# Second expert stream started at the middle expert, and the gates' power issued early in its step

## The chip, the cores and the metric

The kernel runs on one core of one Trainium2 chip. The metric is device time in microseconds of that core, the median of several executions. For the kernel before, three executions took 743.41, 747.35 and 751.59 us; the median is 747.35 us.

## The reference, cut to what matters

Chunked attention makes x, and a router with one expert for each token (top 1) is applied to it.

```python
# attention: q, k, v are (8, 8, 576, 64); chunks of 64 keys, softmax inside a chunk
x = attn_out.transpose(0, 2, 1, 3).reshape(4608, 512)
# router and experts: w1 is (8, 512, 1024), w2 is (8, 1024, 512)
logits = norm(x) @ norm(expert_emb).T / tau
expert_idx = argmax(logits, axis=1)
gate_w = softmax(logits)[row, expert_idx]
for e in range(8):
    mask = expert_idx == e
    out[mask] = gate_w[mask, None] * (relu(x[mask] @ w1[e]) @ w2[e])
```

With the inputs that are used, the experts 0 to 7 get 832, 359, 183, 448, 512, 1023, 576 and 675 tokens. In groups of G = 64 tokens, the last of an expert filled up, that is 13, 6, 3, 7, 8, 16, 9 and 11 groups, 73 in all. These counts were worked out from the reference, not read from a trace.

## The kernel before, in words

**First phase.** Attention, logits and the choice of the expert run tile by tile (128 tokens). Every token's row, with its logits, its squared norm and its number, is scattered to a table `spots` in DRAM, in which each expert has a stretch of its own.

**Second phase, in steps.** A step j takes two groups of 64 tokens, one of each of two streams: stream 0 in partitions 0 to 63, stream 1 in 64 to 127. In the first NE = 4 steps both streams take groups at the start of one expert's stretch, fixed in the program: expert 0 for stream 0 and expert E-1 = 7 for stream 1 (`load_first`, `first_rows`, and `ends_e`, which marks the two experts whose first four groups are done). All groups left over, in the order of their experts, are then walked from both ends: stream 0 from the first upwards, stream 1 from the last downwards (`groups`, `places`). For stream 1, `e_0` is the expert of the first four steps, and `swap` at step 4 is set where the expert of step 4 is another. With the counts above stream 0 walks its experts 0, 1, 2, 3, 4 and changes at steps 13, 19, 22 and 29; stream 1 walks 7, 6, 5 and changes at steps 11 and 20. There are 36 steps of two groups and one of a single group (`step_alone`).

**One step.** The two matrix products of a step are done with seven block products in place of eight. `hidden_fast(j)` (L394) makes the first (L408, products p1 to p7, in six PSUM banks that are reused in turn), with the sums of results on VectorE (`add`, L438), the ReLUs on ScalarE (L425) and the 32x32 transposes on VectorE (`turn`, L432). `result_fast(j)` (L466) makes the second (L485), adds on VectorE (L499), scales by the gate on ScalarE (L511) and scatters the rows to the output from GpSimd (`put_rows`, L543). The sums of x and of h that the seven products need are made by GpSimd (`add_x`, `add_h`, L377).

**The loop (L1267).** The loop's turn j, called turn j below, issues `hidden_fast(j + 1)` and inside it, through `middle()`, `result_fast(j)`. The callbacks fix the order on every engine: `first()` after p1, then a copy of p1 on ScalarE (L442, once a turn, a good clock of the turns), `then()`, p2, `turn_next()` (transposes x of step j+2, issues the loads of step j+4), the other products, and `middle()` after the last of them.

**Changing the expert.** The products use `w1_sb`, `w2_sb` and three sums of weight blocks for each stream (`sums_sb`, `sums2_sb`). The next expert's weights wait in `next_w1` and `next_w2`. For a change at step J, `take_next(J)` in turn J-2 (inside `change`, which `middle` calls last) and `take_next2(J, s)` bring the new weights into use: each has copies on ScalarE (L341, L350), three subtractions of 128x1024 on VectorE and one on GpSimd (L333); `take_next2` has one GpSimd copy more (L353). `take_next2` runs in turn J-1 for stream 0 (inside `change`), and in turn J for stream 1 (inside `then`). All of it stands under run-time conditions (`tc.If`, L339, L348, L359), whose flags each engine loads and tests. After the loop's turn in which `next_w1` was taken, `load_behind(n, next_w1, ...)` (L192, L1323) fetches the weights that come after; `then` does so for `next_w2`. These are loads of 2 MB with a run-time condition, in SyncE's queue, in which the loads of x and of `spot2` stand too.

**Gates.** For every four steps j, j+1, j+2, j+3 with j a multiple of 4, `gates_of_four(j)` (L242) makes the gates in four parts: a power on GpSimd (L254, 128x8) that reads the `spot2` slots of the four steps, five VectorE instructions (L256 to L262), an exponential on ScalarE (L264), and four VectorE instructions (L266 to L269). `middle()` issues the first two parts, before `change(j)`; the rest comes after `hidden_fast`.

Of the kernel before, what the change touches and what calls it, by code (L numbers as in the profile page):

```python
# [13 lines left out]
ALU = mybir.AluOpType  # L14
# [11 lines left out]
def kernel(  # L26
# [11 lines left out]
    nc = tc.nc  # L38
    B, H, S, Dh = q.shape
    E, D = moe_expert_emb.shape  # L40
# [7 lines left out]
    G = P // 2  # L48
# [5 lines left out]
    NE = 4  # L54
# [7 lines left out]
    GB = 4  # L62
# [64 lines left out]
    def load_first(buf, rows):  # L127

        for s in range(2):
            e = (0, E - 1)[s]  # L130
            nc.sync.dma_start(out=whole(buf[s]), in_=rows[:, e : e + 1, :], max_dma_last_dim=4096)

    xin, mo = {}, {}

    def number(ap, top, *engines):
# [34 lines left out]
    def load_x(j):  # L174
        rows = []
        for s in range(2 if j != LEAST else 1):
            row = number(src_row[of_step(s, j)], SPARE, ENG.SP)
            rows.append(spots[ds(row, G), :])
        load_rows(j, rows)

    def first_rows(s, j, n):
        r0 = (0, E - 1)[s] * R + G * j
        return spots[r0 : r0 + G * n, :]

    def load_when(w, rows, e, f):
# [6 lines left out]
    def load_behind(j, place, rows):  # L192

        c = LEAST - 2 - j
        for s in range(2):
            at = (slice(G * s, G * s + 1), slice(c, c + 1))
            load_when(place[s], rows, after[at], more_e[at])
# [44 lines left out]
    def gates_of_four(j):  # L242

        i0 = j % SPOTS2
        sp = spot2[:, i0 : i0 + GB].rearrange("p j b e -> p (j b) e")
        n = 2 * GB
        wide = [P, n, E]
        rn, lmax, sh = g_rn, g_max, g_sh
        place = (j // GB) % 2
        gate, at2 = gates2[:, place], at2s[:, place]  # L250
        for i in range(GB):
            at = slice(2 * i, 2 * i + 2)
            gate_of[j + i] = gate[:, at], at2[:, at]
        nc.gpsimd.tensor_tensor(rn, sp[:, :, SQ], half, ALU.pow)  # L254
        yield
        nc.vector.tensor_reduce(lmax, sp[:, :, 0:E], axis=AX.X, op=ALU.max)  # L256
        nc.vector.tensor_scalar(rn, rn, 1e-6, None, ALU.add)
        nc.vector.reciprocal(rn, rn)
        nc.vector.tensor_tensor(
            sh, sp[:, :, 0:E], lmax.unsqueeze(2).to_broadcast(wide), ALU.subtract  # L260
        )
        nc.vector.tensor_tensor(sh, sh, rn.unsqueeze(2).to_broadcast(wide), ALU.mult)  # L262
        yield
        nc.scalar.activation(sh, sh, AF.Exp)  # L264
        yield
        nc.vector.tensor_reduce(gate, sh, axis=AX.X, op=ALU.add)  # L266
        nc.vector.tensor_scalar(gate, gate, 1e-9, None, ALU.add)
        nc.vector.reciprocal(gate, gate)
        nc.vector.tensor_scalar(at2, sp[:, :, TOK].bitcast(I32), 2.0, odd_q, ALU.mult, ALU.add)  # L269
# [291 lines left out]
    with (  # L561
# [63 lines left out]
        def constant_parts():  # L625
            nc.gpsimd.iota(io_i, pattern=[[1, NST]], base=0, channel_multiplier=0)
            nc.gpsimd.iota(part_i, pattern=[[0, 1]], base=0, channel_multiplier=1)
            nc.gpsimd.memset(blank, 0.0)
            nc.gpsimd.memset(blank[:, D + TOK : D + TOK + 1].bitcast(I32), NO_ROW)
            yield  # L630
            make_upper_triangular(nc, sltb, val=1.0, diag=False)
            nc.gpsimd.memset(onesb, 1.0)
            nc.gpsimd.tensor_copy(io, io_i)
            nc.gpsimd.tensor_copy(at, part_i)
            yield
            nc.gpsimd.tensor_scalar(pref, io[:, 0:E], -1.0, float(E), ALU.mult, ALU.add)
            nc.gpsimd.tensor_scalar(e_base, io[:, 0:E], float(R), None, ALU.mult)
            nc.gpsimd.memset(before, 0.0)
            nc.gpsimd.memset(eqb_all[:, 0], 0.0)
            nc.gpsimd.memset(ones, 1.0)  # L640
            yield
            nc.gpsimd.memset(jump[:, 1], 1.0)
            nc.gpsimd.memset(nb[:, 0:1], float((SPARE + R) // G))
            yield
            nc.gpsimd.tensor_scalar(second, at, float(G), None, ALU.is_ge)
            nc.gpsimd.tensor_scalar(is_0, at, 2.0, None, ALU.is_lt)
            yield
            nc.gpsimd.tensor_scalar(lim, at, -float(P), float(G * NE), ALU.mult, ALU.add)
            nc.gpsimd.tensor_scalar(step, second, -2.0, 1.0, ALU.mult, ALU.add)
            yield  # L650
            nc.gpsimd.tensor_scalar(first_s, second, -1.0, 1.0, ALU.mult, ALU.add)
            nc.gpsimd.tensor_scalar(back, io, -1.0, float(NST - 1), ALU.mult, ALU.add)
            yield
            nc.gpsimd.tensor_scalar(more_g, back, float(LEAST - NE), None, ALU.is_ge)
            nc.gpsimd.tensor_scalar(pair_g, back, float(LEAST - NE), None, ALU.is_equal)
            yield
            nc.gpsimd.tensor_tensor(more_g, more_g, pair_g, ALU.add)
            nc.gpsimd.tensor_tensor(pair_g, back, more_g, ALU.subtract)
            yield
            nc.gpsimd.memset(more_e[:, NSW - 1 : NSW], 1)  # L660
            nc.gpsimd.tensor_scalar(e_0, second, float(E - 1), None, ALU.mult)
            yield
            nc.gpsimd.tensor_scalar(e_1, e_0, 1.0, None, ALU.add)
            nc.gpsimd.tensor_scalar(ends_e, io[:, 0:E], 0.0, None, ALU.is_equal)
            yield
            nc.gpsimd.tensor_scalar(full, io[:, 0:E], float(E - 1), None, ALU.is_equal)
            nc.gpsimd.tensor_tensor(ends_e, ends_e, full, ALU.add)
            yield
            nc.gpsimd.tensor_scalar(done, ends_e, float(NE), None, ALU.mult)
            nc.gpsimd.tensor_scalar(ends_e, ends_e, is_0, None, ALU.mult)  # L670
            yield
            nc.gpsimd.tensor_scalar(in_g, second, -float(G), at, ALU.mult, ALU.add)
            nc.gpsimd.tensor_scalar(odd_q, in_g, float(Q), None, ALU.is_ge)
            nc.gpsimd.tensor_scalar(e_p, second, float(R), None, ALU.mult)
            yield
            nc.gpsimd.tensor_scalar(
                base_h, io[:, 0 : E // 2], 2.0 * R, e_p, ALU.mult, ALU.add
            )
# [564 lines left out]
    spot2 = late_p.tile([P, SPOTS2, 2, E + 2], FP32, name="spot2")  # L1243

    load_x(NE)

    with (
        tc.tile_pool(name="ps_h", bufs=1, space=PSUM, reuse_waits="tile") as ps_h,
# [18 lines left out]
        for j in range(LEAST - 1):  # L1267
            n = j + 2

            def first():  # L1270
                next(ended, None)

            def then():
                if NE <= j:
                    take_next2(j, 1)
                    load_behind(j, next_w2, w2_rows)

            def turn_next():
                next(ended, None)
                if n <= LEAST:  # L1280
                    turn_xb(n)
                if n < LEAST and n + XBUF < NJ:
                    load_x(n + XBUF)

            def middle():
                nonlocal ended, four
                if n < LEAST:
                    add_x(n)
                if NE <= j:
                    if j % GB == 0:  # L1290
                        four = gates_of_four(j)
                        next(four)
                        next(four)
                    ended = result_fast(j, ps_y)
                    next(ended)
                change(j)

            if j == 0:
                first_parts()
                add_up(0, None, TS)  # L1300
                first_parts()
            elif j == 1:
                turn_next()
                add_x(n)
                add_up(1, None, TS)
                hidden_plain(2, w1_sb, lambda s: add_up(s, None, ("T3",)))
            else:
                hidden_fast(j + 1, ps_h, first, then, turn_next, middle)
                for _ in four:
                    pass  # L1310

            if j < NE:
                result(j, ps_y)
                if j >= 2:
                    add_up(j - 2, None, TS, block2)
                if j == NE - 1:
                    for s in range(2):
                        add_up(s, None, ("T3",), block2, nc.gpsimd)
                    take_next2(NE, 0)
            if by_sevens(j + 1):  # L1320
                add_h(j + 1)
            if NE - 1 <= n < LEAST - 1:
                load_behind(n, next_w1, w1_rows)  # L1323
            elif n == LEAST - 1:
                load_late(LEAST, next_w1, w1_rows)
            if j == 1:
                load_behind(NE - 1, next_w2, w2_rows)
# [78 lines left out]
```

## Time and profile before

| what | value |
|---|---|
| median of three executions | 747.35 us |
| the profiled execution | 704.9 us |
| its span, first to last instruction | 703.0 us |
| mean granted TensorE clock in it | 0.965 |
| busy: TensorE matmul / VectorE / ScalarE / GpSimd | 88% / 67% / 53% / 60% |
| start of L442 in turn 2 / in turn 34 | 203.1 / 661.7 us |
| weight loads issued by SyncE (L188), with a condition each | 134 |

A line of a view names start, duration, engine, source line, operation, output and inputs; in brackets stands how long the engine was idle before it and what ended that. In the view of waits, each line names who waited for whom, then the total in us, the number of times and the longest. The sequencer of an engine is written with a q (DVEq): waiting, branching and issuing are its work. DVE is VectorE, ACT ScalarE, PE TensorE, POOL GpSimd, SP SyncE.

### The profile page before, as it was taken

The numbers are of one execution on the slowest core, as the hardware profiler recorded it, in microseconds if no ns is written. First come the engines' busy times: TensorE is split into PE (matmuls) and PEld (weight loads), VectorE is DVE, ScalarE is ACT, GpSimd is POOL, SyncE is SP. The second block draws the span as 40 slices with busy tenths as digits, with TensorE's granted clock in tenths as the row PEclk, the third lists the DMA queues.
The fourth block names the chain that finished last, engine by engine and source line by source line (L and its number), as shares of the span: only waits on it lengthen the run. The fifth ranks groups of instructions, "written<-read, shape, count | busy, mean of one in ns | idle before, by whom it ended". The sixth has DMA issues, their size and how long they took to land. (4 is left out here: it accounts for less than half of the span.)

```text
span 703.0 us, 36397 instructions
## 1 busy us (share of the span) xinstructions
PE 619.4 (88%) x14864; PEld 502.1 (71%) x14864; DVE 469.4 (67%) x1097; ACT 374.9 (53%) x691; POOL 422.8 (60%) x563
## 2 busy tenths in 40 slices
PE   4989899988999899988869999587899998899981
PEld 3878787875445688766649997463699996689971
DVE  2868788884987465576765667886756675765640
ACT  4657676762135365464636566453564755465630
POOL 5749888723442766456766567774666667555631
PEclk9999999999999999999999999897999999799997
DMA  9989999989349121114732114313331111111111
GB/s 227 231 245 272 263 280 277 299 302 389 102 160 390 41 58 40 40 44 156 276 111 95 41 55 160 133 39 131 106 115 38 55 46 34 34 55 38 35 49 31
DMA packets 95468, 96.52 MB, mean 137 GB/s; under 512 B 57788, under 2 KB 77500, under 8 KB 95272
## 3 DMA queue, kind: packets, MB, share of 16 engines
q1 hardware_dynamic: 83032, 55.86, 26.0%
q0 software_dynamic: 12208, 38.04, 16.5%
q8 instruction: 121, 1.98, 1.2%
q14 instruction: 75, 0.61, 0.3%
q10 hardware_dynamic: 32, 0.02, 0.0%
HBM read 328.21 MB, written 22.69 MB: 499 GB/s over the span
## 5 line engine op out<-in xcount | busy, mean ns | idle before, releaser
L425 ACT ACTIVATE h<-C 64x256 f32<-64x256 f32 x264 | 180.7, 684 | 150.6 <-DVE C L438 142.7
L438 DVE TENSOR_TENSOR C<-C,h 128x256 f32<-128x256 f32 x231 | 93.4, 416 | 58.5 <-ACTq L359 22.2
L543 POOL DMA_INDIRECT out_dram<-y,at2s x64 | 63.5, 992 | 83.4 <-ACT y L511 43.4
L408 PE MATMUL h<-sums,xbT 128*32 128x256 f32 x1056 | 81.7, 385 | 8.8 <-DVEq L339 5.5
L485 PE MATMUL y_ps<-w,hT 128*32 128x128 f32 x2048 | 71.3, 291 | 20.4 <-DVE y L499 20.4
L377 POOL TENSOR_TENSOR S<-hT 128x256 f32<-128x256 f32 x64 | 47.0, 735 | 67.3 <-DVE gates L266 20.4
L485 PEld LDWEIGHTS y_ps<-w,hT 128*32 128x32 f32 x2048 | 65.2, 118 | 26.3 <-DVE y L499 23.8
L408 PE MATMUL h<-w,S 128*32 128x256 f32 x1056 | 80.8, 385 | 2.1 <-POOL S L377 1.6
L485 PE MATMUL y_ps<-w,S 128*32 128x128 f32 x2048 | 76.2, 275 | 4.3 <-POOLq L348 3.1
L432 DVE STREAM_TRANSPOSE hT<-h 128x512 f32<-128x512 f32 x66 | 46.7, 707 | 42.9 <-ACT h L425 34.3
L408 PE MATMUL h<-w,xbT 128*32 128x256 f32 x1056 | 69.6, 385 | 5.5 <-ACT w L341 2.9
L485 PE MATMUL y_ps<-sums,hT 128*32 128x128 f32 x2048 | 67.4, 277 | 2.6 <-DVE sums L333 2.4
L485 PEld LDWEIGHTS y_ps<-w,S 128*32 128x32 f32 x2048 | 64.3, 111 | 6.1 <-POOLq L348 3.9
L499 DVE TENSOR_TENSOR y<-y,y_ps 128x128 f32<-128x128 f32 (+1 forms) x192 | 56.1, 306 | 18.7 <-PE y_ps L485 11.1
L408 PEld LDWEIGHTS h<-sums,xbT 128*32 128x32 f32 x1056 | 45.8, 111 | 28.6 <-issue 8.2
L485 PEld LDWEIGHTS y_ps<-sums,hT 128*32 128x32 f32 x2048 | 61.1, 112 | 3.5 <-DVE sums L333 2.9
L408 PEld LDWEIGHTS h<-w,S 128*32 128x32 f32 x1056 | 47.0, 112 | 19.1 <-POOL S L377 2.6
L408 PEld LDWEIGHTS h<-w,xbT 128*32 128x32 f32 x1056 | 43.6, 111 | 20.3 <-ACT w L341 4.0
L930 POOL DMA_INDIRECT spots<-xr,dest x36 | 37.5, 1041 | 25.7 <-DVE dest L895 8.5
L209 DVE STREAM_TRANSPOSE xbT<-xin 128x256 f32<-128x256 f32 x73 | 45.5, 658 | 0.1
L702 POOL DMA_DIRECT2D kx<-in_k_dram x36 | 32.0, 891 | 19.7 <-PE tr L725 19.1
L408 PE MATMUL h<-sums,S 128*32 128x256 f32 x528 | 42.2, 393 | 0.0
(231 smaller groups left out, 1185.0 us busy)
## 6 DMA issues: line engine op xcount, KB each, us to landing
next_w<-in_moe_w_dram SPq DMA_DIRECT2D x134, 2048.0 KB
xin<-spots SPq DMA_DIRECT2D x154, 64.0 KB
qx<-in_q_dram POOLq DMA_DIRECT2D x32, 256.0 KB
w<-in_moe_w_dram SPq DMA_DIRECT2D x4, 2048.0 KB
v<-in_v_dram SPq DMA_DIRECT2D x56, 144.0 KB
kx<-in_k_dram POOLq DMA_DIRECT2D x28, 256.0 KB
spot<-spots SPq DMA_DIRECT2D x128, 2.5 KB
spots<-blank SPq DMA_DIRECT2D x9, 144.0 KB
```

The source lines that it names most:

```text
L209: nc.vector.transpose(xT[:, :, cols].rearrange("p c (b i) -> p b c i", i=Q), t[:, s * (D // 2) : (s + 1) * (D // 2)].rearrange("p (b i c) ...
L377: nc.gpsimd.tensor_tensor(o, a, b, op)
L408: nc.tensor.matmul(ps[t0 : t0 + Q], lhsT=a[:, c, s], rhs=w[:, r], start=c == 0, stop=c == KD // 2 - 1,)
L425: nc.scalar.activation(h[b][G * v : G * v + G, s].rearrange("p (k i) -> p k i", i=Q), x[G * s : G * s + G].rearrange("p (i k) -> p k i", i=Q),
L432: nc.vector.transpose(hT.rearrange("p k (s b i) -> p b s k i", b=2, i=Q)[:, b], h[b].rearrange("p s (k i) -> p s k i", i=Q),)
L438: nc.vector.tensor_tensor(out, a, b, op)
L485: nc.tensor.matmul(o[t0 : t0 + Q], lhsT=a[:, c, s], rhs=block2(s, m)[:, c, r], start=c == 0, stop=c == KF // 2 - 1,)
L499: nc.vector.tensor_tensor(out, a, b, ALU.add)
L543: ins = nc.gpsimd.indirect_dma_start(out=to, out_offset=bass.IndirectOffsetOnAxis(ap=at, axis=0), in_=y, in_offset=None, bounds_check=boun ...
L702: eng.dma_start(out=x[done : done + n], in_=src[b, :, s : s + n, :].rearrange("h p d -> p h d"),)
L930: ins = nc.gpsimd.indirect_dma_start(out=spots, out_offset=bass.IndirectOffsetOnAxis(ap=at, axis=0), in_=m, in_offset=None, bounds_check=S ...
```

## The change

Three edits, made together. First, the fixed expert of stream 1 becomes E // 2 = 4 wherever E - 1 stood for it. Second, `load_behind(NE - 1, next_w1, ...)` moves from the end of turn 1 to a place ahead of the loop. Third, the generator of the gates is made in `first()`, which issues its GpSimd power there; `middle()` goes on with its VectorE part.

The walk over the left-over groups from both ends stays as it is. Stream 1 now takes four groups of expert 4 and then begins at the last expert, so that with the counts above it walks 4, 7, 6, 5 and changes at steps 4, 15 and 24. Stream 0 walks 0, 1, 2, 3, 4, 5 and changes at steps 13, 19, 22, 29 and 33.

```diff
     def load_first(buf, rows):
         for s in range(2):
-            e = (0, E - 1)[s]
+            e = START[s]
...
+    START = 0, E // 2
...
     def first_rows(s, j, n):
-        r0 = (0, E - 1)[s] * R + G * j
+        r0 = START[s] * R + G * j
...
-            nc.gpsimd.tensor_scalar(e_0, second, float(E - 1), None, ALU.mult)
+            nc.gpsimd.tensor_scalar(e_0, second, float(START[1]), None, ALU.mult)
...
-            nc.gpsimd.tensor_scalar(full, io[:, 0:E], float(E - 1), None, ALU.is_equal)
+            nc.gpsimd.tensor_scalar(full, io[:, 0:E], float(START[1]), None, ALU.is_equal)
...
     load_x(NE)
+    load_behind(NE - 1, next_w1, w1_rows)
...
             def first():
+                nonlocal four
+                if NE <= j and j % GB == 0:
+                    four = gates_of_four(j)
+                    next(four)
                 next(ended, None)
...
             def middle():
-                nonlocal ended, four
+                nonlocal ended
                 if n < LEAST:
                     add_x(n)
                 if NE <= j:
-                    if j % GB == 0:
-                        four = gates_of_four(j)
-                        next(four)
-                        next(four)
+                    next(four, None)
                     ended = result_fast(j, ps_y)
                     next(ended)
                 change(j)
...
-            if NE - 1 <= n < LEAST - 1:
+            if NE <= n < LEAST - 1:
                 load_behind(n, next_w1, w1_rows)
```

## Prediction

> **What bounds the kernel now.** I read the busy shares first: TensorE 88%, VectorE 67%. The loop of turns was therefore to be measured turn by turn, and the copy L442 on ScalarE, one in each turn, gives the clock. Lines of ScalarE's timeline, turns 24, 25, then 28 to 31:
>
> ```profile
> 528.12 0.37 ACT L442 COPY C<-h 128x256 f32<-128x256 f32 x1 [2.29 <-PE h L408]
> 540.28 0.37 ACT L442 COPY C<-h 128x256 f32<-128x256 f32 x1 [0.79 <-PE h L408]
> ...
> 577.86 0.38 ACT L442 COPY C<-h 128x256 f32<-128x256 f32 x1
> 593.47 0.38 ACT L442 COPY C<-h 128x256 f32<-128x256 f32 x1
> 613.08 0.37 ACT L442 COPY C<-h 128x256 f32<-128x256 f32 x1 [1.83 <-PE h L408]
> 625.26 0.37 ACT L442 COPY C<-h 128x256 f32<-128x256 f32 x1 [2.03 <-PE h L408]
> ```
>
> A quiet turn takes 540.28 - 528.12 = 12.16 us, and there TensorE is busy throughout (12.20 of 12.20 us from 528.5 to 540.7). Turns 28 and 29, about the change of stream 0 at step 29, take 15.61 and 19.61. Over all turns from 4 to 33 the excess over 12.16 us is: turn 4, 3.3; turn 8, 1.3; turns 9 and 10, 7.0 (stream 1 changes at 11); turns 11 to 13, 14.5 (the rest of that, and stream 0 at 13); turns 17 to 22, 31.1 (changes at 19, 20, 22); turns 27 to 29, 11.9 (change at 29). That is 69.1 us; the rest of the loop is bound by TensorE. The turns 16, 24 and 32 make gates too and have no excess.
>
> Next, who waits. From the view of waits:
>
> ```profile
> PE y_ps L485 <- DVE y L499: 20.4, 6, 7.2
> DVE g_rn L257 <- POOL g_rn L254: 19.3, 8, 3.3
> ```
>
> TensorE stands still because VectorE is late with y, and VectorE waits 2.4 us for the gates' power, eight times. The timeline about the change at 29 joins the two:
>
> ```profile
> 588.47 0.18 DVE L256 TENSOR_REDUCE g_max<-spot 128x8 f32<-128x64 f32 x1
> ...
> 589.77 1.67 POOL L254 TENSOR_TENSOR g_rn<-spot,halves 128x8 f32<-128x8 f32 x1
> ...
> 591.47 0.17 DVE L257 TENSOR_SCALAR g_rn<-g_rn 128x8 f32<-128x8 f32 x1 [2.82 <-POOL g_rn L254]
> ...
> 595.06 1.49 DVE L333 TENSOR_TENSOR sums<-next_w 128x1024 f32<-128x1024 f32 x1 [2.84 <-DVEq L339]
> ...
> 602.98 3.64 PE L485 MATMUL y_ps<-w,hT 128*32 128x128 f32 x64 [3.37 <-DVE y L499]
> ```
>
> VectorE loses 2.82 us to the power, 2.84 to its conditions, some 4.6 to the three subtractions, and only then makes hT and y. TensorE then waits 3.37 us and runs its next 64 matmuls in 3.64 us, against 1.92 in a quiet turn. Turn 4 is another case, GpSimd late with two first subtractions:
>
> ```profile
> 229.43 4.74 POOL L333 TENSOR_TENSOR w<-w 128x1024 f32<-128x1024 f32 x2
> 234.35 0.72 POOL L377 TENSOR_TENSOR S<-hT 128x256 f32<-128x256 f32 x1 [0.18 <-POOLq L348]
> ```
>
> **What the Trainium skill says.** "TensorE: Matmul & The Clock Gate", section "Part 1: The HAM clock gate", says that the array drops to half clock after an idle window of about 3.4 us; the trace agrees (mean granted clock 0.74 from 593.5 to 613.1, the 64 matmuls above), so a stall costs more than its length. "SBUF — State Buffer", section "SBUF: two separate sides", says that a VectorE instruction with two SBUF inputs and a GpSimd one exclude each other; the trace agrees (L333 takes 1.22 to 3.37 us on VectorE and 2.36 to 3.38 on GpSimd). "Runtime: NRT & Kernel Launch", section "Instruction fetch mechanics", says that a taken branch can force a fetch; the 2.84 us at L339 fit, but no row here shows the cause.
>
> **The change, part by part.** I price it by changes of an expert, and the prices come from the table above.
>
> *Stream 0, with the power early.* The change at 29 cost 11.9. With the power issued in `first`, GpSimd makes it after `add_h`, some 3.4 us into the turn, while it has 5 us free (6.78 of 12.20 busy). VectorE then goes through L257 at once, and its chain to y is 2.8 earlier; TensorE is bound by that chain, so 2.8 is gained whole: 9.1. It can be worked out the other way: y would end at 600.2, where TensorE without the stall at 593.5 would want it at about 595; 5.2 of stall, 2.9 of half clock until 608.7, and 1.0 in turn 27 make 9.1. Where no gates are made in the turn, about 1.9 us less VectorE work (nine small instructions) stands in the way: 7.2. The changes 13, 29 and 33 end in turns 12, 28 and 32 with gates; 19 and 22 do not.
>
> *Stream 1.* `take_next` delays TensorE by 1.35 (copies of w, at 305.0) and then 1.27 (y, at 312.9); with the half of 7.0 that the gates of turn 8 already cost VectorE, I take 4. `take_next2` in `then` made TensorE wait 2.38 at 331.7 for the subtractions, with some half clock: 3.5. Together 7.5. Bounds: 4, if VectorE's spare 5.3 us of a turn (6.87 of 12.20 busy) take most of it, and 10.
>
> *Step 4, new.* The subtractions of expert 4's w2 in turns 3 and 4 are still made, and thrown away. In turn 4 GpSimd has the two first subtractions until 234.2, `add_h` until 237.5, now the power (1.7), the condition (1.1), then `take_next2`'s subtraction (2.4 to 3.3): done at 242.7 to 243.6. TensorE wants it as third product of `result_fast(4)` at about 234.6. The stall is 8 to 9 us against 2.7 before; with 1.7 to 3.4 of half clock behind it, and about 1 from `take_next(4)` in turn 2, where three subtractions delay VectorE by some 5 us, mostly behind the 7.0 us of plain products (L525), turn 4 loses 9.5 more than before. Bounds 5 and 14. The copy of 2.0 us after it hides behind three products of 0.87.
>
> *The load moved ahead.* Two issues of about 1.6 us and 2 x 2 MB at the 415 GB/s seen from 205 to 228 us: landed near 201 us, if the buffers are free at 191. SyncE's queue is passed by nothing but the loads of step 5, whose transposes come at 216.9, and `take_next(4)` reads at about 212: hidden. Without it the weights of step 4 would land at 214 or later. As the weights no longer come as 8 MB in one stretch, x of steps 6 and 7 comes some 10 us earlier, and VectorE's wait of 4.66 at 240.3 for `spot2` goes; it was hidden by GpSimd's lateness in part. Two more changes mean 4 x 2 MB more, at 5 us each beside quiet turns: nothing.
>
> *Waits added.* The power in `first` now waits for `spot2` of step j+3, loaded in turn j-1, and behind it on GpSimd stand `put_rows`, `add_x` and so L408's third product. SyncE is busy for about 11.9 of 12.16 us in a turn, and in turn 8 it was a turn late: `spot2` landed at 290.2, 10.6 into the turn. There GpSimd stands about 6 us and its rows and `add_x` come 0 to 2 us late; against that goes the excess of 1.3. I take 0 left in turn 8; bounds 0 and 3.
>
> Sum of the excess after: turn 4, 3.3 + 9.5 = 12.8; stream 0, 3 x 9.1 + 2 x 7.2 = 41.7, and 1 for the gates in turn 20; stream 1, 2 x 7.5 = 15; 2 more where a change of one stream follows on the tail of the other's (13 to 15, 21 to 24). In all 72.5, against 69.1: 3.4 us more, on the execution of 704.9. The median of the runs is 42 us above that execution, and nothing in the trace tells me where; I add the same 3 us to it: 750 us.
>
> So the split of the streams is worth little by these prices: three changes in turns 17 to 22 cost 31.1, and the prices of single ones would give 11.9 + 7.5 + 9.1 = 28.5. What is gained by the power (8.4 at three changes and 1.3 at turn 8) pays for less than two new changes.
>
> **Rivals.** *The overlap was dear.* If changes that stand alone fall into the spare 5 us of VectorE and 5 of ScalarE, those without gates cost perhaps 4 rather than 7, and the half clock seldom comes. Then 3 x 6 + 2 x 4 + 2 x 4 + 12 = 46, 23 less than before: 725 us. For it: three subtractions at 1.23 are under the spare time. Against it: the change at 29 stood alone. Halfway, 736.
>
> *Step 4 is dear (the other side).* One mechanism: GpSimd in turn 4. If its subtraction meets VectorE's (3.3 rather than 2.4, for all three), it ends at 246, and VectorE's own chain, 5 us late from turn 2, ends after that; stall 11.5, and half clock for 6.8 us. Turn 4 then loses 14 rather than 9.5, and the result is 755; from 13.5 on the kernel is over 1% slower if the other changes stay at their prices of 9.1 throughout (stream 0 at 45.5), which gives 760.
>
> *The change does not do what it says.* If `spot2` is late in turns 8, 16 and 20, the early power holds GpSimd and VectorE waits as before: 8 us worse than my sum, 758. Against it: at 16 and 24 the loads had landed when VectorE asked (it waited for the power alone).
>
> **How the numbers follow.** Little net change (743 to 754): 0.42, with its own range 742 to 755. Dear overlap, whole or half: 0.25, 725 to 740. Dear step 4: 0.20; late loads: 0.13; both reach 755 to 765. About 1%, 7.5 us, is what a measurement tells from no change. Faster by more than that: 0.26; within: 0.38, as part of the first case spills on both sides; slower: 0.36. The range for 8 in 10 is 733 to 765.
>
> **What would show it.** Right: VectorE's wait for L254 falls from 19.3 to near 0; `take_next` at L333 on GpSimd counts 16 rather than 12; turn 4 takes 22 to 28 us with TensorE waiting for POOL at L485; turns 9 and 10 take 12.2; turns 31 to 33 have an excess of 9. Wrong: turn 4 under 19 us, or lone changes at 15, 24 and 33 with an excess under 4 each, or GpSimd waiting over 3 us at L254.

## The result, and the profile after

| what | before | after |
|---|---|---|
| median of 20 runs each | 747.29 us | 751.46 us |
| lowest and highest run | 742.68, 752.26 | 748.39, 755.35 |
| profiled execution, its span | 704.9, 703.0 us | 748.75, 746.8 us |
| mean granted TensorE clock | 0.965 | 0.967 |

The ratio is 1.0056 [1.0031, 1.0081]: within 1%, 4.2 us more, and inside the range. All ratios here are worked out from the fast executions alone, as a few are slow at a lower clock, and so differ by up to about half a point (0.01 of a ratio is a point) from the quotients of the medians. The two profiles, though, are not of one kind, and this has to be read first. ScalarE's timeline of the kernel after, the clock copy (now L445; lines after the first edit moved by three), turns 25 to 27 and then 29 to 31:

```profile
564.92 0.37 ACT L445 COPY C<-h 128x256 f32<-128x256 f32 x1 [1.71 <-PE h L411]
578.33 0.37 ACT L445 COPY C<-h 128x256 f32<-128x256 f32 x1 [2.88 <-PE h L411]
591.71 0.37 ACT L445 COPY C<-h 128x256 f32<-128x256 f32 x1 [2.93 <-PE h L411]
...
621.53 0.38 ACT L445 COPY C<-h 128x256 f32<-128x256 f32 x1
640.85 0.37 ACT L445 COPY C<-h 128x256 f32<-128x256 f32 x1 [2.42 <-PE h L411]
654.32 0.37 ACT L445 COPY C<-h 128x256 f32<-128x256 f32 x1 [2.98 <-PE h L411]
```

A quiet turn takes 13.41 us here (564.92 to 578.33), where the profile of before had 12.16. The view of waits of the same kernel shows in which product the 1.25 us lie (who waited for what, total us, times, longest):

```profile
PE y_ps L488 <- issue: 29.2, 67, 1.2
...
PE y_ps L488 <- DVE y L502: 18.2, 8, 4.3
...
PE y_ps L488 <- POOL w L336: 10.4, 2, 7.7
```

"Issue" means that TensorE waited for nothing that the profile shows. The 29.2 us are less than 33 turns x 1.25 us = 41, but the place is right: in the quiet turn from 578.33 the first 64 matmuls of L488 last from 583.19 to 586.16, 2.97 us, where they take 1.75 in a quiet turn of after_again (551.41 to 553.16), the same kernel on another chip (below). That run has quiet turns of 12.16 us, and in its view of waits stands:

```profile
PE y_ps L488 <- issue: 1.7, 2, 1.0
```

There the kernel before has a median of 708.35 us, 39 less than in the table, against those 41 us. That is the likely answer to what the prediction left open, why the runs took 42 us more than the profiled execution: it was made on another chip than they. This is inferred. The record gives no chip number for the runs of the table, and no profile of the kernel before has turns of 13.4 us; why such turns wait is not known. Turns are compared below between profiles with quiet turns of 12.16 us, unless the text says otherwise.

The lines about the change at step 29, kernel after, its timeline:

```profile
616.34 0.29 DVE L260 TENSOR_SCALAR g_rn<-g_rn 128x8 f32<-128x8 f32 x1
...
620.34 1.23 DVE L336 TENSOR_TENSOR sums<-next_w 128x1024 f32<-128x1024 f32 x1 [2.59 <-PE y_ps L488]
621.04 2.76 POOL L336 TENSOR_TENSOR w<-next_w 128x1024 f32<-128x1024 f32 x1 [2.29 <-DMA spot<-spots]
621.67 5.18 DVE L336 TENSOR_TENSOR sums<-next_w,sums 128x1024 f32<-128x1024 f32 x2
...
630.05 3.64 PE L488 MATMUL y_ps<-w,hT 128*32 128x128 f32 x64 [4.18 <-DVE y L502]
```

VectorE's wait of 2.82 us for the power is gone, but the two later subtractions take 5.18 us, with GpSimd's subtraction (2.76 us) beside them. TensorE still waits 4.18 us for y. Turn 4 of the kernel after, on GpSimd and TensorE:

```profile
241.80 5.89 POOL L336 TENSOR_TENSOR w<-w 128x1024 f32<-128x1024 f32 x2
...
247.88 1.47 POOL L380 TENSOR_TENSOR S<-hT 128x256 f32<-128x256 f32 x1 [0.18 <-POOLq L351]
...
253.43 1.68 POOL L257 TENSOR_TENSOR g_rn<-spot,halves 128x8 f32<-128x8 f32 x1
255.10 2.35 POOL L336 TENSOR_TENSOR w<-next_w 128x1024 f32<-128x1024 f32 x1
...
257.50 1.71 PE L488 MATMUL y_ps<-w,S 128*32 128x128 f32 x26 [7.69 <-POOL w L336]
```

This is the order that was foreseen: first sums, sums of h, power, subtraction, and TensorE standing still for 7.69 us until the last. Turn 4 takes 24.3 us.

### The profile page after: what moved, and what is told of

Read it like the earlier page. It is cut to its first block, busy times and chain, and to the rows that moved or that the text cites. A ratio compares the mean times of both kernels' runs of the same rounds, so it can differ in the third digit from the quotient of the medians.

```text
span 746.8 us, 36513 instructions
## 1 busy us (share of the span) xinstructions
PE 636.8 (85%) x14864; PEld 535.5 (72%) x14864; DVE 504.8 (68%) x1109; ACT 384.7 (52%) x701; POOL 439.7 (59%) x569
## 3 DMA queue, kind: packets, MB, share of 16 engines
q1 hardware_dynamic: 85144, 64.25, 27.7%
## 5 line engine op out<-in xcount | busy, mean ns | idle before, releaser
L441 DVE TENSOR_TENSOR C<-C,h 128x256 f32<-128x256 f32 x231 | 93.4, 416 | 66.7 <-ACTq L362 15.3
L488 PE MATMUL y_ps<-w,hT 128*32 128x128 f32 x2048 | 79.1, 284 | 31.8 <-DVE y L502 18.2
L488 PEld LDWEIGHTS y_ps<-w,hT 128*32 128x32 f32 x2048 | 65.9, 114 | 45.2 <-DVE y L502 22.5
L488 PE MATMUL y_ps<-w,S 128*32 128x128 f32 x2048 | 82.5, 283 | 18.1 <-POOL w L336 10.4
L488 PE MATMUL y_ps<-sums,hT 128*32 128x128 f32 x2048 | 77.2, 277 | 14.3 <-issue 14.2
L488 PEld LDWEIGHTS y_ps<-w,S 128*32 128x32 f32 x2048 | 68.5, 114 | 21.6 <-POOL w L336 10.9
L488 PEld LDWEIGHTS y_ps<-sums,hT 128*32 128x32 f32 x2048 | 64.6, 112 | 22.0 <-issue 21.1
L411 PEld LDWEIGHTS h<-sums,xbT 128*32 128x32 f32 x1056 | 55.1, 110 | 6.5
L336 POOL TENSOR_TENSOR w<-next_w 128x1024 f32<-128x1024 f32 x16 | 48.9, 3054 | 18.2 <-PE h L411 6.9
L411 PEld LDWEIGHTS h<-w,S 128*32 128x32 f32 x1056 | 55.1, 110 | 6.3
L411 PEld LDWEIGHTS h<-w,xbT 128*32 128x32 f32 x1056 | 50.7, 110 | 6.6 <-issue 1.2
L336 DVE TENSOR_TENSOR sums<-next_w,sums 128x1024 f32<-128x1024 f32 x24 | 54.1, 2255 | 1.2
```

The costliest lines, as they stand in the source:

```text
L336: eng.tensor_tensor(of(s, o), of(s, a, w), of(s, b, w), ALU.subtract)
L411: nc.tensor.matmul(ps[t0 : t0 + Q], lhsT=a[:, c, s], rhs=w[:, r], start=c == 0, stop=c == KD // 2 - 1,)
L441: nc.vector.tensor_tensor(out, a, b, op)
L488: nc.tensor.matmul(o[t0 : t0 + Q], lhsT=a[:, c, s], rhs=block2(s, m)[:, c, r], start=c == 0, stop=c == KF // 2 - 1,)
```

## The experiments

The theory going in: each change of an expert has its price, separating the streams saves little, and the two added changes (steps 4 and 33) are paid by the early power. The rival: that the overlap of changes was dear, and the change gained there what it lost elsewhere. Several chips were used, each run beside the kernel before on its own chip (medians 707.8 to 708.4 us, quiet turns of 12.16 us in every profile). The excess is what turns take over 12.16 us each, in one profiled execution.

**before_again**: no edit.

> The kernel before, unchanged, for a second profile of it. In the profile of after a quiet turn takes 13.4 us and TensorE waits some 1.2 us in each for 'issue' at L488; in the profile of before it took 12.16. Theory: that wait belongs to the execution and not to the change, so this profile shows quiet turns of about 13.4 us and a span near 745 us. Rival: the change itself slowed the quiet turns, so this profile shows 12.16 us again and a span near 703 us. The time is about 747 us by either.

716.58 us in one run, beside a median of 707.79, and quiet turns of 12.16 us. The time of 747 us was expected by both theories and did not come. That it is not the change that makes quiet turns long is shown by after_again, below. The excess over turns 4 to 33 is 73.0 us, where the first profile had 69.3; most of the longer time was lost before the loop (turn 2 starts at 210.56 us, not 203.1). A single profile of one kernel thus varies by some 4 us in this sum, and differences below that in one profile prove nothing.

**power_only, split_only, no_idle_sums**, together. The first is the third edit alone on the kernel before:

```diff
             def first():
+                nonlocal four
+                if NE <= j and j % GB == 0:
+                    four = gates_of_four(j)
+                    next(four)
...
             def middle():
...
-                    if j % GB == 0:
-                        four = gates_of_four(j)
-                        next(four)
-                        next(four)
+                    next(four, None)
```

> Only the third edit: the gates' power in first(), with stream 1 still starting at expert 7 and the load where it was. Theory (the sum of the prediction): 2.8 us gained at each of the three changes whose turn makes gates (turns 12, 20, 28) and 1.3 at turn 8, so about 738 us, ratio 0.987. Rival 1 (the power only moves the wait to GpSimd's other work): 747 us. Rival 2 (the gain of the whole change comes from the split, and the power does harm in turns with late loads): over 747 us.

704.38 us, ratio 0.995 [0.9926, 0.9973], where the theory had 0.987. The power early is a gain by itself, but less than half of that expected, as turn 4 takes 22.37 us (16.55 in before_again). Its timeline there:

```profile
243.83 1.68 POOL L254 TENSOR_TENSOR g_rn<-spot,halves 128x8 f32<-128x8 f32 x1 [3.39 <-DMA next_w<-in_moe_w_dram]
245.61 1.71 PE L485 MATMUL y_ps<-w,S 128*32 128x128 f32 x26 [7.12 <-POOLq L348]
```

GpSimd stands 3.39 us; the profile names the load of weights, behind which the rows for the power stand in SyncE's queue. TensorE stands 7.12 us for GpSimd to pass a condition (L348) whose block it does not even enter. The rival of the late loads is real, where the weight load is not moved ahead.

split_only is the first two edits, with the power left in `middle()` (here against the kernel after):

```diff
...
             def middle():
...
                 if NE <= j:
-                    next(four, None)
+                    if j % GB == 0:
+                        four = gates_of_four(j)
+                        next(four)
+                        next(four)
```

> The first two edits without the third: stream 1 starts at expert 4, the load stands ahead of the loop, the power stays in middle(). Theory: two more changes of an expert, less what the overlap had cost, 747 + 13 = 760 us, ratio 1.017; of that about 9 in turn 4. Rival (overlap was dear): the split alone is not slower than before, 740 to 749 us.

724.57 us, ratio 1.0186 [1.0122, 1.025], as expected. no_idle_sums is the kernel after without the first sums of stream 1's second weights, which nothing reads:

```diff
-                if j >= 2:
-                    add_up(j - 2, None, TS, block2)
+                if j == 2:
+                    add_up(0, None, TS, block2)
                 if j == NE - 1:
-                    for s in range(2):
-                        add_up(s, None, ("T3",), block2, nc.gpsimd)
+                    add_up(0, None, ("T3",), block2, nc.gpsimd)
```

> The changed kernel without the first sums of stream 1's second weights (three subtractions on VectorE in turn 3, one on GpSimd), which are overwritten before use as stream 1 changes at step 4 with these inputs. Theory: in turn 4 GpSimd is what TensorE waits for (7.69 us at L488), so the stall shrinks by the 2.4 to 2.9 us of the subtraction and by VectorE's 3.7 us that block it: turn 4 takes about 18 us and not 24, and the time is about 746 us. Rival: VectorE's lateness from turn 2 sets the stall, and turn 4 keeps 22 us or more: 750 us.

718.12 us, ratio 1.0157 [1.0108, 1.0206]; turn 4 takes 21.2 us, between the two that were expected, where the kernel after takes 24.5 (after_again). But the long stall did not shrink, as the theory had it:

```profile
246.18 1.71 PE L488 MATMUL y_ps<-w,S 128*32 128x128 f32 x26 [8.08 <-POOL w L336]
```

It is 7.68 us in after_again. What went are two shorter waits ahead of it, 1.89 and 1.73 us there and 0.35 here. The first sums are part of turn 4's price, not all of it.

**after_again, load_only, power_and_load, start_at_5**, together on a third chip. after_again has no edit.

> The changed kernel, unchanged, so that it can be compared on the chip of these runs. Where quiet turns take 12.16 us, theory: the first prices hold in full, sum of the excess about 72 us against 69 for before, ratio 1.005. But the split alone measured 1.0186 and the power alone 0.995; if these add, 1.0186 - 0.005 = 1.0136. Rival (the early power is worth its full 8 to 10 us only beside the moved load): 1.005.

722.57 us, ratio 1.0217 [1.0176, 1.0259]: 14.2 us more than before, where the table above has 4.2, and more than either expectation (1.0136 and 1.005). The size of the effect differs between the two chips.

load_only is the second edit alone on the kernel before, shown here; power_and_load is the kernel after with `START = 0, E - 1`, that is, the second and third edits:

```diff
     load_x(NE)
+    load_behind(NE - 1, next_w1, w1_rows)
...
-            if NE - 1 <= n < LEAST - 1:
+            if NE <= n < LEAST - 1:
```

> Only the second edit: the load of the next first weights ahead of the loop, power in middle(), stream 1 from expert 7. Theory: VectorE's wait for spot2 in turn 4 goes, but GpSimd is late there all the same, so 0 to 2 us: ratio 0.997 to 1.000. Rival: the late loads are what makes turn 4 long, 4 us and more: 0.994.

705.96 us, ratio 0.9974 [0.995, 0.9998], as expected.

> The second and third edit without the split: stream 1 from expert 7, six changes. With the power alone turn 4 took 22.4 us against 16.6, as GpSimd waited 3.4 us at L254 for spot2 and TensorE 7.1 us for GpSimd. Theory: with the load moved that wait goes and the power gains its whole 8 to 10 us: ratio 0.986 to 0.989, turn 4 about 16 us or less. Rival (the power is worth 0.5% with or without the load): 0.995.

699.82 us, ratio 0.9903 [0.9876, 0.993], though turn 4 takes 18.73 us and not the 16 of the theory. Without the split the change is a gain of about 1%. The split is what costs: 3.1 points beside the other two edits, 2.1 between load_only and split_only, which ran on different chips.

start_at_5 is the kernel after with `START = 0, E // 2 + 1`, so that stream 0 has no change at step 33, while the others stand at 13, 19, 22, 29 and 4, 15, 24 as before:

> The changed kernel with stream 1 started at expert 5 rather than 4. With these inputs stream 0 then walks 0 to 4 and changes at 13, 19, 22, 29, and stream 1 walks 5, 7, 6, 5 and changes at 4, 15, 24: the same schedule as the changed kernel without stream 0's change at 33, and still no two changes in the same turns. Theory (each change has its price): 9 us faster than the changed kernel, ratio 1.2 points under that of after_again; turns 31 to 33 take 12.16 us each. Rival (what counts is that streams change apart; the number of changes is cheap): within 2 us of after_again.

712.1 us, ratio 1.0052 [1.0028, 1.0076]. One change less is 10.5 us less than after_again; the excess of turns 31 to 33 in after_again was 10.4. Now the groups of turns:

| excess, us | turn 4 | 5 to 16 | 17 to 24 | 27 to 29 | 31 to 33 | sum |
|---|---|---|---|---|---|---|
| before_again | 4.4 | 24.5 | 33.3 | 10.8 | 0 | 73.0 |
| load_only | 2.7 | 22.8 | 33.1 | 10.8 | 0 | 69.5 |
| power_and_load | 6.6 | 15.9 | 26.6 | 10.6 | 0 | 59.7 |
| predicted for after | 12.8 | 17.6 | 23.9 | 9.1 | 9.1 | 72.5 |
| split_only | 12.1 | 21.3 | 31.1 | 11.9 | 10.6 | 86.0 |
| after_again | 12.4 | 19.1 | 27.7 | 11.4 | 10.4 | 80.9 |

Three changes stand close in power_and_load (19, 20, 22: 26.6 us) and apart in after_again (19, 22, 24: 27.7); with the power late they cost 33.1 close (load_only) and 31.1 apart (split_only). The rival of the dear overlap, which was to save 23 us, falls.

The early power takes 7 us each from turns 5 to 16 and 17 to 24 where stream 1 starts from expert 7 (load_only against power_and_load). Where it starts from expert 4 (split_only against after_again) it takes 2.1 and 3.5, 5.1 us over all turns, and the two ratios, 1.0186 and 1.0217, show no gain at all. And in neither does it take anything clear of the variation from a change that stands alone, in turns 27 to 29 or 31 to 33. Why not is read in two timelines of one chip, which differ by the third edit. First load_only:

```profile
590.92 0.18 DVE L256 TENSOR_REDUCE g_max<-spot 128x8 f32<-128x64 f32 x1
...
593.92 0.17 DVE L257 TENSOR_SCALAR g_rn<-g_rn 128x8 f32<-128x8 f32 x1 [2.82 <-POOL g_rn L254]
...
595.54 2.35 POOL L333 TENSOR_TENSOR w<-next_w 128x1024 f32<-128x1024 f32 x1 [1.66 <-DMA spot<-spots]
...
597.51 1.46 DVE L333 TENSOR_TENSOR sums<-next_w 128x1024 f32<-128x1024 f32 x1 [2.84 <-DVEq L339]
...
599.08 3.13 DVE L333 TENSOR_TENSOR sums<-next_w,sums 128x1024 f32<-128x1024 f32 x2
602.13 0.70 DVE L432 STREAM_TRANSPOSE hT<-h 128x512 f32<-128x512 f32 x1
```

Then power_and_load:

```profile
585.11 0.18 DVE L259 TENSOR_REDUCE g_max<-spot 128x8 f32<-128x64 f32 x1
585.21 0.28 DVE L260 TENSOR_SCALAR g_rn<-g_rn 128x8 f32<-128x8 f32 x1
...
589.30 1.23 DVE L336 TENSOR_TENSOR sums<-next_w 128x1024 f32<-128x1024 f32 x1 [2.69 <-PE h L411]
...
589.90 2.87 POOL L336 TENSOR_TENSOR w<-next_w 128x1024 f32<-128x1024 f32 x1 [2.30 <-DMA spot<-spots]
...
590.64 5.20 DVE L336 TENSOR_TENSOR sums<-next_w,sums 128x1024 f32<-128x1024 f32 x2
...
595.75 0.70 DVE L435 STREAM_TRANSPOSE hT<-h 128x512 f32<-128x512 f32 x1
...
599.03 3.22 PE L488 MATMUL y_ps<-w,hT 128*32 128x128 f32 x56 [6.14 <-DVE y L502]
```

From the reduction of the gates to the first subtraction VectorE takes 6.59 us with the power late (597.51 - 590.92) and 4.19 with the power early (589.30 - 585.11): 2.4 of the 2.8 us arrive. But with the power late, GpSimd's subtraction began 2 us ahead of VectorE's first, while VectorE waited, and it was done when VectorE's second began. Now it begins inside the first, and VectorE's second and third take 5.20 us rather than 3.13. Of 2.4 us, 2.1 are gone again, and hT, which the next product needs, is made only 0.6 us earlier (10.64 after the reduction, not 11.21).

The kernel after has the same. At the change of step 33, split_only, then after_again:

```profile
664.60 2.36 POOL L336 TENSOR_TENSOR w<-next_w 128x1024 f32<-128x1024 f32 x1 [1.67 <-POOLq L342]
...
668.15 3.12 DVE L336 TENSOR_TENSOR sums<-next_w,sums 128x1024 f32<-128x1024 f32 x2
```

```profile
659.53 2.95 POOL L336 TENSOR_TENSOR w<-next_w 128x1024 f32<-128x1024 f32 x1 [2.29 <-PE h L411]
660.35 5.20 DVE L336 TENSOR_TENSOR sums<-next_w,sums 128x1024 f32<-128x1024 f32 x2
```

At steps 13 and 29 the two subtractions of after_again take 5.18 and 5.19 us.

**power_late_at_4, vector_w2, vector_both** start from power_and_load, on a fourth chip. The last two test this meeting of the engines, the first what turn 4 costs. In it the power of step 4 alone goes back to `middle()`:

```diff
             def first():
-                if NE <= j and j % GB == 0:
+                if NE < j and j % GB == 0:
...
             def middle():
...
                 if NE <= j:
+                    if j == NE:
+                        four = gates_of_four(j)
+                        next(four)
                     next(four, None)
```

> Power early and load early with stream 1 from expert 7, but the power of step 4 alone goes back into the middle of its turn. If the power of step 4 holds GpSimd until the rows of step 7 have landed, and that alone makes turn 4 take 18.7 us rather than the 14.9 of the kernel with only the load moved, then turn 4 goes back to about 15 and the kernel gains 3.8 us over the same kernel with all powers early (0.990): ratio 0.985, turns 5 to 33 unchanged. If TensorE in turn 4 waits for something else that the load or the condition makes late, turn 4 stays at 18 to 19 us: ratio 0.990.

697.67 us, ratio 0.9847 [0.9808, 0.9886], which overlaps with that of power_and_load; the excess in the profile, 61.0, is no smaller than its 59.7. Turn 4 takes 17.39 us, neither 15 nor 18.7. The stall of TensorE fell from 3.67 to 2.05, by about the power's 1.68. What remains over load_only's 14.90 are two things that the timelines show: an indirect DMA issue ahead on GpSimd took 1.92 us rather than 0.99, and 60 matmuls after the stall took 3.44 us rather than 1.90, at a mean granted clock of 0.51. The last stall is as long in both (2.05 us here, 2.04 in load_only), but here another, of 0.92 us, ended 0.4 us before it. The Trainium skill ("TensorE: Matmul & The Clock Gate", section "Part 1: The HAM clock gate") calls the window over which the activity is counted free-running, about 3.4 us long. With that, the first stall or the place of both in the window can have made the difference; no run here parts the two. Whether the power at step 4 should be late stays open.

vector_w2 makes all four subtractions of the second weights on VectorE, and GpSimd's copy on ScalarE; vector_both moves the fourth subtraction of the first weights too (only vector_both has the part in `take_next`):

```diff
 def take_next(j):
...
-                add_up(s, next_w1, ("T3",), eng=nc.gpsimd)
+                add_up(s, next_w1, ("T3",))
...
 def take_next2(j, s):
...
-            add_up(s, next_w2, ("T3",), block2, nc.gpsimd)
-            nc.gpsimd.tensor_copy(block2(s, "B22"), block2(s, "B22", next_w2))
+            add_up(s, next_w2, ("T3",), block2)
+            nc.scalar.copy(block2(s, "B22"), block2(s, "B22", next_w2))
```

> Power early and load early with stream 1 from expert 7; the fourth subtraction of the second weights' sums is made on VectorE rather than on GpSimd, and the copy that GpSimd made, on ScalarE. If the overlap of GpSimd's subtraction with VectorE's is what eats the gain of the early power (the second and third subtraction of VectorE took 5.20 us together at the change of step 29, against 3.12 where GpSimd had finished earlier), four subtractions on VectorE take 4 x 1.23 = 4.9 us against 6.4 for three: hT comes 1.5 us earlier at each of those changes, and with TensorE's half clock after the stall some 1.5 to 2 us a change: 5 to 9 us over six changes, ratio 0.978 to 0.984; turns 28 and 29 together 2 us shorter. If the two do not disturb each other, and VectorE is simply slow there, the fourth subtraction adds 1.3 to 1.6 us a change: 8 us more, ratio 1.001.

689.97 us, ratio 0.9772 [0.9728, 0.9816]. The time is what was expected, but partly by luck: the excess of turns 5 to 29, with all six changes, falls by 2.4 us (53.2 to 50.8) where 5 to 9 were expected, and turn 4, of which nothing was said, by 5.4.

> As the kernel with the second weights' fourth subtraction on VectorE, and the fourth subtraction of the first weights' sums on VectorE too. If the overlap is the cause in both places, VectorE's four take 4.9 us in the turn two before the change as well, against 3.7 to 6 for three beside GpSimd: 0 to 1 us gained a change, ratio 0.975 to 0.984. If VectorE is bound by its own work there, each of six changes costs 1.2 us more than in the kernel with only the second weights' subtraction moved: 7 us, 0.01 more in ratio than that kernel.

687.61 us, ratio 0.9712 [0.9679, 0.9746], the lowest of all kernels here, though its interval meets that of vector_w2. The same place of vector_both:

```profile
575.28 0.16 DVE L260 TENSOR_SCALAR g_rn<-g_rn 128x8 f32<-128x8 f32 x1
...
579.29 1.23 DVE L336 TENSOR_TENSOR sums<-next_w 128x1024 f32<-128x1024 f32 x1 [2.86 <-DMA spot<-spots]
580.63 2.49 DVE L336 TENSOR_TENSOR sums<-next_w,sums 128x1024 f32<-128x1024 f32 x2
583.03 1.22 DVE L336 TENSOR_TENSOR w<-next_w 128x1024 f32<-128x1024 f32 x1
...
587.45 3.64 PE L488 MATMUL y_ps<-w,hT 128*32 128x128 f32 x64 [4.57 <-DVE y L502]
```

Four subtractions end 4.96 us after the first began, where three beside GpSimd's took 6.54. The second and third take 2.49 us with nothing on GpSimd, 3.13 beside its copy alone (load_only, 597.84 to 599.87) and 5.20 beside its subtraction and the copy: most of the loss is the subtraction's. More work on the engine that sets the time, and the time is shorter: the excess of turns 27 to 29 falls from 10.6 to 8.0 us. The idle time ahead of the first, 2.86 us, is nearly as long in all three profiles (2.84, 2.69) and has a different releaser named in each (DVEq L339, PE, a DMA). What they have in common are the conditions of `change` between the gates and the subtractions; that these make the wait was not tried.

Not all of the gain comes from there. Over turns 5 to 29 it is 5.0 us in the profiles of power_and_load and vector_both, and turns 9 to 13 gained nothing (15.9 to 17.5). As much, 5.2 us, comes from turn 4, which I had not expected: 18.73 to 13.49. TensorE there, power_and_load, then vector_both:

```profile
244.10 0.96 PE L488 MATMUL y_ps<-w,S 128*32 128x128 f32 x26 [3.67 <-POOLq L351]
```

```profile
238.67 1.08 PE L488 MATMUL y_ps<-w,S 128*32 128x128 f32 x32 [0.72 <-POOL S L380]
```

No change takes place there, but GpSimd had the condition of `take_next2` to pass, behind the power, and TensorE waited 3.67 us for that. With no GpSimd instruction left in the block, only the wait for the sums of h is left.

**split_vector_both** is vector_both with `START = 0, E // 2`.

> The changed kernel (stream 1 from expert 4) with the fourth subtractions of both weights' sums on VectorE and GpSimd's copy on ScalarE. If GpSimd's work at a change, which overlaps VectorE's subtractions and comes late in turn 4, makes up much of the price of the two added changes, then a change costs about 8 us as in the kernel with stream 1 from expert 7 (49.5 us of excess for six), turn 4 falls from 24.5 to about 18, and the two more changes add 8 + 6 = 14 us to the 0.971 of that kernel: ratio 0.991, and 3 points below the changed kernel's 1.022. If the split is dear for another reason (more loads, more conditions), change 33 still takes 10.4 us and turn 4 still 24: 0.971 + 23/708 = 1.003. If the two streams' overlapping changes were the greater cost, the split would gain here: below 0.971.

701.67 us, ratio 0.9884 [0.9837, 0.9931]: 3.3 points below after_again, as the first theory has it. The excess of turns 31 to 33 is 8.6 us (10.4 in after_again), that of turn 4 is 9.4 (12.4). For turn 4, 5.8 were expected; TensorE still waits 2.30 us for a copy, 1.73 for a sum and 3.76 for VectorE's fourth subtraction. Turns 5 to 29 together have 42.5 us of excess, those of vector_both 48.2, while after_again has 58.1 and power_and_load 53.2, split_only 63.3 and load_only 66.7. So separating the streams gains 6 us with GpSimd out of the changes, cost 5 with GpSimd in and the power early, and gained 3, less than one profile varies, with the power late. The added changes at 4 and 33 cost 16.7 more in split_vector_both, and the split loses in all three.

## Why the prediction was right, and where its working was not

**The time.** 751.46 against 750.0, and +4.2 us against +3.4. But the sum was worked out on a profile with quiet turns of 12.16 us, and on the chips that have these the change costs 14.2 us. The sum was 8.4 us short in excess there (80.9 against 72.5). On the slower chip the excess of the kernel after over its own quiet turn of 13.4 us is 61 us, and the lone changes cost 8.9 each (turns 27 to 29 and 31 to 33), near the 9.1 of the prediction. Yet there too VectorE's two subtractions take 5.18 us at step 29. VectorE has 1.25 us more of each turn there; that this is what makes the changes cheaper is a guess, and was not tried. What the kernel before has there is not known, as no profile of it has such turns. So the close hit is in part luck: the changes came dearer than priced, and the chip of the runs made the difference smaller.

**The step that failed** is that of stream 0: "its chain to y is 2.8 earlier; TensorE is bound by that chain, so 2.8 is gained whole: 9.1". On the chips of the profile it measured 11.4 at turns 27 to 29 of after_again and 10.6 in power_and_load, against 10.8 and 11.9 in the two profiles of before: nothing gained, within what one profile varies. In power_and_load 2.4 us of the 2.8 came, and 2.1 were lost to GpSimd's subtraction, which the late power had kept out of VectorE's way. The prediction had named the cause and used it for turn 4, and did not ask the same of the change at 29: the Trainium skill ("SBUF — State Buffer", section "SBUF: two separate sides") says that a VectorE instruction with two SBUF inputs and a GpSimd one exclude each other, and here VectorE's two take 5.20 us beside GpSimd's work and 2.49 without. What it moved was not only VectorE's start but the order of two engines. At the change of step 33 the price was 10.4, again not 9.1 (10.6 with the power late, in split_only).

**The gain of the power as a whole** was taken as 9.7 us (8.4 and 1.3). load_only and power_and_load differ by 9.8 us in excess, but not where it was put: 6.9 in turns 5 to 16, 6.5 in 17 to 24, 0.2 at the change of 29, and 3.8 lost in turn 4. In medians it is 6.1 us. In the changed kernel, for which it was priced, it is 5.1 us in excess and not seen in the ratios. The two edits were added up, and their gains do not add; why turns 5 to 24 gain more where the streams' changes meet was not sought.

**Stream 1's prices** and those without gates: turns 5 to 16 19.1 against 17.6, turns 17 to 24 27.7 against 23.9. The five changes there came about 1 us dearer each than priced, on average, in the same direction as the failed step.

**Turn 4** was right in size: 12.4 us of excess against 12.8. Its stall was 7.68 us for w, 1.89 for a copy and 1.73 for a sum (after_again), instead of 8 to 9 for w alone; GpSimd's two first subtractions took 5.90 us, not the 4.74 of before, since VectorE's sums ran beside them.

**The load moved ahead** was hidden, as costed: ratio 0.9974 for it alone, if anything a gain. It shortened turn 2, which the sum leaves out, from 11.64 to 9.74 us.

**The separation of the streams** was priced at a gain of 2.6 us (31.1 against 28.5). With the power late it is 2.0 us in turns 17 to 24 (33.1 to 31.1), with the power early a loss of 1.0; neither is clear of what one profile varies. The reason given, that each change has its price, holds; start_at_5 shows it most plainly.

**The wait added**: GpSimd's power in turn 8 waits 3.48 us for the rows in the profile after (4.16 in after_again), over the 3 that the prediction gave as a sign of being wrong. It cost 0.7 us in that turn in after_again, where 0 was taken and 3 was the bound. The sign was set too low, since 5 us of GpSimd were free.

**The half clock.** The prediction read the trace as agreeing with the idle window of about 3.4 us that it takes from the Trainium skill. The stall of 3.37 us that it shows does (granted clock 0.50 from 602 to 608 us). But in the same profile half clock (0.50 from 596 to 598 us) also came after a stall of 2.34 us, ended at 593.47, and one of 0.18 behind four matmuls. The measurement decides: here less than 3.4 us of idle time was enough.

**Other signs.** The wait of 19.3 us at the gates is gone; GpSimd's subtraction of the next weights counts 16; turns 9 and 10 take 12.16 us in after_again; turns 31 to 33 have an excess of 8.9 or 10.4. Of the rivals, late loads were real only without the second edit, and dear overlap did not show. Turn 4 lost 9.1 us more than in the first profile (12.4 against 3.3), below the 13.5 of the dear step 4.

## What to carry to other kernels

When a wait is taken off one engine, list what other engines did during that wait: an engine that shares a resource may have used it, and comes back into the way when the wait is gone. Work moved from a helper engine to the engine that bounds the time can pay, if the two exclude each other anyway (four subtractions in 4.96 us, against three in 6.54), and if it takes the helper out of a condition that others must see passed. Two gains that were priced one by one need not add: the early power was worth 0.7 points with one order of the experts, and none that the ratios show with the other. Before a sum is made on a profile, see whether its time is that of the runs: 1.25 us a turn were most likely the 42 us that nothing in the trace explained.

## What the runs showed of the hardware

- Chips seem to differ: one profile had 29.2 us of waits for "issue" at TensorE's second product, another 1.7 for the same kernel, with quiet turns of 13.41 and 12.16 us at granted clocks of 0.967 and 0.956. The same change is 0.6% slower in one set of runs and 2.2% in the other. That the chip makes this, and not some lasting state of it, is not shown.
- In these kernels a condition whose block is not entered still holds those who wait for what the block would write: 3.67 us of TensorE behind GpSimd in turn 4 of power_and_load, 7.12 in power_only. Without GpSimd's instructions in the block the wait was gone.
- VectorE idles 2.6 to 2.9 us between the gates and the subtractions, where it passes the conditions of `change`, whatever releaser the profile names.
- Two VectorE subtractions of 128x1024 took 2.49 us alone, 3.13 beside a GpSimd copy, and 5.20 where a GpSimd subtraction was under way too.
